# Longer score runs, and DMA transposes in place of TensorE transposes, in a fused attention and squared-ReLU kernel

## The chip, the cores and the metric

The kernel runs on one core of a Trainium2 chip. Times are device microseconds of one execution of the whole program; the median of several runs is the time of a kernel. The core has a matrix engine (PE), a vector engine (DVE), an activation engine (ACT), a general engine (POOL) and a queue engine (SP). In this program POOL issues the loads from HBM, and SP issues the constants and the stores. All of these DMAs run on the same 16 DMA engines.

## The reference

Eight batches, eight heads, 576 positions, head width 64. Attention with a bias that depends only on the distance of two positions, then a two-layer network with a squared ReLU on every token:

```python
scores = q @ k^T / 8 + bias_table[bucket(|i - j|)]        # 8 x 8 x 576 x 576
attn   = softmax(scores)
x      = (attn @ v), heads side by side                   # 4608 tokens x 512
out    = relu(x @ w_in) ** 2 @ w_out                      # 512 -> 2048 -> 512, fp32
```

All distances of 128 and more share one bucket. So only a band around the diagonal needs a factor of its own, and the kernel multiplies exp(score) by a small table there.

## The kernel before, in words

The work is cut in 32 **pairs**: pair p is batch p/4 and heads 2·(p%4) and the next one. The two heads lie on the two halves of the 128 partitions.

- **Loads.** q and k of a batch are loaded into a staging buffer `stg` (two of them), positions on the partitions, and cast to fp16. v goes to `vas` and `v4s`.
- **Turning q and k.** `pair` turns them with five 128x128 PE transposes each (L504) into a PSUM bank of the ring `g_ps` (three banks). ACT or DVE copies the bank to `qts` and `kts` (L483, L485).
- **Scores.** For each block of 128 keys (four blocks) and each half of 288 queries, two matmuls of 64x128 tiles, one per head, write one of two PSUM sets `sets_ps` (L528). The 64 last keys take four matmuls of 64x64 tiles (L535). ACT takes the exponential of each set into `pts` or `p4s` (L554), two buffers of each. DVE multiplies the band by the table (L574).
- **Attention times v** ("PV"): five tiles of 128 queries in two parts (three and two tiles). Each tile is one matmul of 130 columns (L612) and eight of 65 (L619). DVE divides by the sum (L636, L641) and writes `xs`.
- **Turning x.** After the four pairs of a batch `x_turn` turns x with 20 PE transposes (L663) into `xt_sb`, again through `g_ps` and a copy.
- **The network** runs over nine groups of 512 tokens. The first layer has 16 chunks of four 512-column matmuls (`f1`, L758), each followed by a ReLU on ACT (L778) and a square on DVE (L786). The second layer has four output tiles of 16 matmuls (`f2`, L707), each followed by a copy (L727 or L733) and a store (L741). `f1` and `f2` use the same three PSUM banks as the transposes.

Scores use PE as two arrays of 64 rows, and the 64 last keys as 64x64 arrays. Everything else uses it as one array of 128x128. The planner calls these modes "r", "q" and "f".

The order of all instructions is written out by a planner, `Plan.schedule`, when the program is built. It places each step on its engine at the earliest time its inputs and buffers allow, with assumed costs (`mm`, `act`, `dve`), assumed delays between engines (`LAT`), an assumed cost of a change of PE mode (`SWITCH`), and due times (`nominal`, and `due` in `layers`) as a tie break. The chip then runs each engine's instructions in that order.

## Time and profile before

| | |
|---|---|
| three runs | 442.41, 442.55, 440.94 us; median 442.41 us |
| the profiled execution's own time | 443.17 us |
| its span, first to last instruction | 441.4 us |
| busy: PE, ACT, DVE, POOL | 417.2, 288.0, 210.2, 119.5 us |
| granted PE clock, mean | 0.996 |
| first `f1` matmul starts | 50.24 us |
| last matmul ends | 437.6 us |

The profile is of one execution. A group row names a line of the kernel, an engine, an operation, its tiles and its count; then the busy time, the mean length of one, and the idle time of the engine just before. The length of one matmul in it is the time from start to end, and several are in flight at once, so what a matmul costs is read from the distance between starts. The windows view has one row for each stretch of time, with busy time by engine, granted clock and the mean share in which the 16 DMA engines were busy. The timeline view gives start, length and count of instructions in order of time.

### The profile page before, as it was taken

To read this page: it belongs to the slowest core of one execution; us is meant where nothing else is said; L and a number is where in the kernel's file an instruction comes from. 1 tells how busy PE (TensorE), PEld (TensorE's weight loads), DVE (VectorE), ACT (ScalarE), POOL (GpSimd) and SP (SyncE) were. 2 spreads that over 40 slices of the span, in tenths; PEclk is the share of its full clock that TensorE was granted. 3 is DMA by queue.
4 is the path that set the end of the run, shared out by engine and by line. 5 is a ranking of instruction groups with operands and counts; after the bars stand their busy time and mean duration, and the time that the engine had idled before them with its cause. 6 is when DMAs were issued, how large, how long until landed. Compare 5 with 4: busy or idle time off the path is not lost.

```text
span 441.4 us, 9092 instructions
## 1 busy us (share of the span) xinstructions
PE 417.2 (95%) x3713; PEld 209.7 (48%) x3713; DVE 210.2 (48%) x513; ACT 288.0 (65%) x495; POOL 119.5 (27%) x154
## 2 busy tenths in 40 slices
PE   1687999999999999999999999999999999999996
PEld 0265545554455445544454445544454454544442
DVE  3545556445555655455455446465544553352210
ACT  1657787667866876777767666685777766464421
POOL 7998569422162205230254007000000000000000
PEclk9998999999999999999999999999999999999999
DMA  9999999918091808980099009400010001000111
GB/s 131 159 87 165 190 166 122 137 29 76 2 133 28 74 1 74 108 55 24 26 133 79 1 25 113 68 1 25 25 50 1 25 24 49 25 25 25 48 49 72
DMA packets 122170, 29.24 MB, mean 66 GB/s; under 512 B 113896, under 2 KB 117008, under 8 KB 122128
## 3 DMA queue, kind: packets, MB, share of 16 engines
q0 software_dynamic: 115552, 18.36, 56.5%
q1 hardware_dynamic: 6576, 10.30, 6.7%
q8 instruction: 29, 0.48, 0.5%
q14 instruction: 13, 0.11, 0.1%
HBM read 37.55 MB, written 9.45 MB: 106 GB/s over the span
## 4 chain that ended last, share of the span: by engine, by line
PE 91%; DMA 3%; ACT 3%; DVE 2%; issue 1%; SPq 0%; ACTq 0%; DVEq 0%
PE f L707 30%; PE f L758 29%; PE st L528 11%; PE pv L619 9%; PE f L504 4%; PE pv L612 3%; PE st L535 3%; PE f L663 2%; ACT pt L554 2%; DMA tr_sb<-t_bias 1%; DMA t_bias<-tv_sb 1%; DMA oh_sb<-c_oh 1%; SPq L243 0%; DVE pt L574 0%; ACT y L727 0%
## 5 line engine op out<-in xcount | busy, mean ns | idle before, releaser
L554 ACT ACTIVATE pt<-st 128x576 f16<-128x576 f32 x256 | 157.3, 649 | 42.1 <-PE st L528 40.1
L707 PE MATMUL f<-w_out_sb,g 128*128 128x512 f16 x576 | 144.9, 380 | 0.4 <-ACT qt L483 0.3
L758 PE MATMUL f<-xt,w_in_sb 128*128 128x512 f16 x576 | 141.0, 380 | 0.9 <-DVE xt L485 0.4
L778 ACT ACTIVATE rt<-f 128x512 f16<-128x512 f32 x144 | 86.1, 598 | 57.1 <-PE f L758 53.2
L786 DVE TENSOR_TENSOR g<-rt 128x512 f16<-128x512 f16 x144 | 61.1, 425 | 100.6 <-ACT rt L778 100.4
L758 PEld LDWEIGHTS <-w_in_sb 128*128 128x128 f16 x576 | 51.0, 97 | 61.3 <-issue 3.8
L574 DVE TENSOR_TENSOR pt<-pt,tb_sb 128x512 f16<-128x512 f16 (+2 forms) x96 | 59.7, 623 | 40.7 <-ACT pt L554 37.7
L707 PEld LDWEIGHTS <-g 128*128 128x128 f16 x576 | 48.7, 98 | 60.8 <-issue 13.2
L528 PE MATMUL st<-qt,kt 64*128 64x288 f16 x512 | 66.2, 298 | 4.8 <-ACT pt L554 3.7
L243 POOL DMA_DIRECT2D qs<-in_q_dram x47 | 38.1, 834 | 101.4 <-PE f L504 98.1
L619 PE MATMUL pv<-va,pt 128*128 128x65 f16 x1280 | 57.2, 196 | 0.2 <-DVE pt L574 0.2
L619 PEld LDWEIGHTS <-pt 128*128 128x128 f16 x1280 | 52.6, 100 | 5.1 <-issue 0.7
L528 PEld LDWEIGHTS <-kt 64*128 64x128 f16 x512 | 20.2, 94 | 57.8 <-issue 52.9
L243 POOL DMA_DIRECT2D va<-in_v_dram x32 | 28.4, 916 | 43.0 <-PE pv L619 26.9
L243 POOL DMA_DIRECT2D ks<-in_k_dram x47 | 38.2, 858 | 6.3 <-DMA w_out_sb<-in_moe_w_out_dram 3.5
L612 PE MATMUL pv<-vm,pm 128*128 128x130 f16 x160 | 36.1, 225 | 0.2 <-DVE x L641 0.2
L641 DVE TENSOR_TENSOR x<-pv,r 128x384 f16<-128x384 f32 x64 | 31.4, 491 | 2.2
L554 ACT ACTIVATE pm<-st 128x576 f16<-128x576 f32 x32 | 20.8, 651 | 13.0 <-PE st L535 13.0
L636 DVE RECIPROCAL r<-pv 128x6 f32<-128x6 f32 x64 | 11.9, 187 | 26.0 <-PE pv L619 25.7
L727 ACT ACTIVATE y<-f 128x512 f32<-128x512 f32 x20 | 12.0, 598 | 18.6 <-PE f L707 18.2
L504 PE MATMUL f<-id_sb,qs 128*128 128x128 f16 x160 | 15.5, 234 | 4.3 <-DMA qs<-in_q_dram 4.3
L612 PEld LDWEIGHTS <-pm 128*128 128x128 f16 x160 | 15.9, 99 | 6.5 <-issue 1.4
(37 smaller groups left out, 175.7 us busy)
## 6 DMA issues: line engine op xcount, KB each, us to landing
out_dram<-y SPq DMA_DIRECT2D x36, 256.0 KB, 2.0
va<-in_v_dram POOLq DMA_DIRECT2D x32, 128.0 KB, 5.2
qs<-in_q_dram POOLq DMA_DIRECT2D x28, 128.0 KB, 4.6
ks<-in_k_dram POOLq DMA_DIRECT2D x28, 128.0 KB, 5.1
w_in_sb<-in_moe_w_in_dram POOLq DMA_DIRECT2D x4, 512.0 KB, 7.4
w_out_sb<-in_moe_w_out_dram POOLq DMA_DIRECT2D x4, 512.0 KB, 9.5
qs<-in_q_dram POOLq DMA_DIRECT2D x15, 64.0 KB, 4.8
ks<-in_k_dram POOLq DMA_DIRECT2D x15, 64.0 KB, 4.7
```

Source lines behind the costliest of these rows:

```text
L243: lambda: io(eng.dma_start(out=out_(), in_=in_())),
L504: io(nc.tensor.transpose(ps[:, ts(t, 128)], stg[b_stg[b].slot][w][:, t, ts(hp, 128)], id_sb))
L528: nc.tensor.matmul(ps[:, e, 0:HQ], kt[rows, ts(jt, 128)], qt[rows, ts(hh, HQ)], start=True, stop=True,)
L554: nc.scalar.activation(out=dst, in_=sets_ps[st.slot][:, :, 0:HQ], func=EXPF, scale=SCALE)
L574: io(nc.vector.tensor_tensor(out=a, in0=a, in1=t, op=MULT))
L612: nc.tensor.matmul(ps[:, i, :, :], pm[:, c : c + 128], vm[:, hp, :, 0:65], start=True, stop=False)
L619: nc.tensor.matmul(ps[:, i, e, :], pt[:, (2 * jt + e) * S + c : (2 * jt + e) * S + c + 128], va[:, jt, 2 * hp + e, 0:65], start=False, sto ...
L641: nc.vector.tensor_tensor(out=xs[xb.slot][:, qt0 : qt0 + nq, ts(hp, 128)].rearrange("p t (e d) -> p t e d", e=2), in0=ps[:, :, :, 0:64], i ...
L707: nc.tensor.matmul(g_ps[bank.slot], gs[gb.slot][:, nt, ts(m, 128)], w_out_sb[:, nt, :], start=(nt == 0), stop=(nt == 15),)
L758: nc.tensor.matmul(g_ps[bank.slot], w_in_sb[:, kk, ts(nt, 128)], xt_sb[:, kk, c : c + GT], start=(kk == 0), stop=(kk == 3),)
L778: nc.scalar.activation(out=rts[rb.slot], in_=g_ps[bank.slot], func=RELUF)
L786: nc.vector.tensor_tensor(out=gs[gb1.slot][:, nt, :], in0=rts[rb.slot], in1=rts[rb.slot], op=MULT)
```

## The change

The scores of a pair are asked for in fewer and longer pieces. A step `run` multiplies one or two blocks of 128 keys with the first 512 queries at once: two 512-column matmuls of 64x128 tiles per block. From batch 1 on a pair has two such runs, of two key blocks each, and a run takes both PSUM sets together. In batch 0 it has four runs of one block. The remaining 64 queries and 64 keys are computed with the whole array: `spread` copies them into zeroed 128x128 tiles `qzs` and `kzs`, one head in each diagonal corner. `last_queries` then takes four matmuls of 128 columns and `last_keys` two of 288. The exponentials follow: four of 1024 elements per partition, one of 576 and one of 512 per pair, in place of nine of 576.

q and k of batches 2 to 7 are turned by `dma_start_transpose` on SP, from the staging buffer to `qts` and `kts`, five blocks of 128x128 in one DMA. Each part of x is turned by a DMA transpose of three or two blocks as soon as it is divided, from `xs` to `xt_sb`. q and k of batches 0 and 1 are loaded six positions to a partition and turned by PE in 12 transposes of 96 x 64, two beside each other.

The layouts of `stg`, `xs` and `xt_sb` follow this: `xt_sb` holds four batches, and the group of 512 tokens that wraps round its end is computed in two halves of 256 columns. The bias table is staged in a buffer of the network's hidden layer. The loads come in another order: q and k of batch 0 first, the weights later. q and k of batches 2 to 7 are loaded by 20 DMAs a batch in place of 10. The planner gets other costs and due times.

```diff
-XR = 2560
+XR = 4 * S
+DT_QK = 2
+PERIOD, LEAD, FAST, FASTN = 9800.0, 10600.0, 4700.0, 5
+AHEAD, G0, GP = 12700.0, 38500.0, 37900.0
+DT_X = True
...
-LAT = {"PE": 200.0, "ACT": 90.0, "DVE": 90.0, "POOL": 120.0, "DMA": 0.0, "SP": 0.0}
-SWITCH = 60.0
+LAT = {"PE": 200.0, "ACT": 90.0, "DVE": 90.0, "POOL": 120.0, "DMA": 1800.0, "SP": 0.0, "XB": 2000.0}
+SWITCH = 105.0
...
-        t = 0.0
+        t, taken = 0.0, {}
         for b in op.bufs:
             if b.slot is None:
-                if not b.ring.free:
+                i = taken[b.ring] = taken.get(b.ring, -1) + 1
+                if len(b.ring.free) <= i:
                     return float("inf")
-                t = max(t, min(b.ring.free)[0])
+                t = max(t, sorted(b.ring.free)[i][0])
         return t
...
-    NSTG, NQK, NPT, NV, NX, NGB, NRT, NY = 2, 5, 2, 3, 2, 2, 4, 3
-    stg = [[sb(f"{n}s{i}", [128, 5, 512]) for n in "qk"] for i in range(NSTG)]
-    qts = [sb(f"qt{i}", [128, S]) for i in range(NQK)]
-    kts = [sb(f"kt{i}", [128, S]) for i in range(NQK)]
+    NSTG, NQK, NPT, NV, NX, NGB, NRT, NY = 2, 4, 2, 3, 2, 2, 4, 3
+    stg = [[sb(f"{n}s{i}", [128, 6 * 512]) for n in "qk"] for i in range(NSTG)]
+    qts = [sb(f"qt{i}", [128, 640]) for i in range(NQK)]
+    kts = [sb(f"kt{i}", [128, 640]) for i in range(NQK)]
+    qzs = [sb(f"qz{i}", [128, 128]) for i in range(NQK)]
+    kzs = [sb(f"kz{i}", [128, 128]) for i in range(NQK)]
...
-    xs = [sb(f"x{i}", [128, 5, 512]) for i in range(NX)]
-    xt_sb = sb("xt", [128, 4, XR])
+    xs = [sb(f"x{i}", [128, 4, 5, 128]) for i in range(NX)]
+    xt_sb = sb("xt", [128, 4, XR + 64])
     gs = [sb(f"g{i}", [128, 16, GT]) for i in range(NGB)]
+    tr_sb = gs[1][:, 0:6, :].rearrange("p a b -> p (a b)").rearrange("p (h w) -> p h w", h=H)
...
+    def load_six(b, w, h0, nh):
+        src = (q, k)[w]
+        l = load(
+            "POOL", nc.gpsimd,
+            lambda: six(stg[b_stg[b].slot][w])[:, h0 : h0 + nh, :],
+            const(src[b, h0 : h0 + nh].rearrange("h (p j) d -> p h (j d)", j=6)),
+            96 * nh * 107, (), [b_stg[b]], pdue(),
+        )
+        for hp in range(h0 // 2, (h0 + nh) // 2):
+            l_qk[b, w, hp] = [l]
...
+        for hp in range(4):
+            l_qk[b, w, hp] = tails + [
+                load(
+                    "POOL", nc.gpsimd,
+                    lambda hp=hp, e=e: rows(stg[b_stg[b].slot][w])[:, hp, 0:4, ds(64 * e, D)],
+                    const(src[b, 2 * hp + e, 0:512, :].rearrange("(t p) d -> p t d", p=128)),
+                    512 * 34.5, first, [b_stg[b]], pdue(),
+                )
+                for e in range(2)
+            ]
...
     for hp in range(4):
         for w in range(2):
-            load_pair(0, w, hp)
+            load_six(0, w, 2 * hp, 2)
         if hp == 1:
-            load_v(0)
+            load_v_tail(0, range(4))
+            for h in range(4):
+                load_v_head(0, h)
+    for h in range(4, 8):
+        load_v_head(0, h)
+    for u in range(4):
+        load_w_in(u)
     for w in range(2):
-        load_qk(1, w)
-    for kk in range(4):
-        load_w_in(kk)
+        load_six(1, w, 0, 4)
     load_v(1)
+    for w in range(2):
+        load_six(1, w, 4, 4)
     for u in range(4):
         load_w_out(u)
...
-    PERIOD, LEAD, FAST = 10300.0, 12000.0, 5900.0
-
     def nominal(p):
-        return LEAD + FAST * min(p, 5) + PERIOD * max(p - 5, 0)
-
-    xt_ready = {}
+        return LEAD + FAST * min(p, FASTN) + PERIOD * max(p - FASTN, 0)
...
-        after = max(0.0, T - 9000.0)
+        after = max(0.0, T - AHEAD)
         qb = Buf(r_qk)
         evac = []
         for w, dst in ((0, qts), (1, kts)):
+            if b >= DT_QK:
+                o = P.add(
+                    {"SP": 1250.0},
+                    lambda w=w, dst=dst: io(
+                        nc.sync.dma_start_transpose(
+                            out=dst[qb.slot].rearrange("p (t d) -> p t d", d=128), in_=rows(stg[b_stg[b].slot][w])[:, hp].rearrange("p t d -> p (t d)")
+                        )
+                    ),
+                    l_qk[b, w, hp], [qb, b_stg[b]], T - 6000, after,
+                )
+                evac.append(P.add({"XB": 800.0}, None, [o], [qb, b_stg[b]], T - 6000))
+                continue
...
-                for t in range(5):
-                    io(nc.tensor.transpose(ps[:, ts(t, 128)], stg[b_stg[b].slot][w][:, t, ts(hp, 128)], id_sb))
-
-            o = P.add({"PE": 5 * mm(128)}, tr, l_qk[b, w, hp] + [l_id], [bank, b_stg[b]], T - 3000, after, "f")
...
+                if b < SIX:
+                    for j in range(6):
+                        for e in range(2):
+                            io(
+                                nc.tensor.transpose(
+                                    ps[ds(64 * e, 64), ts(j, 96)], six(t)[:, 2 * hp + e, ts(j, D)],
+                                    id_sb[0:96, 0:96],
+                                )
+                            )
+                else:
...
+        spread = []
+        for w, src, dst in ((0, qts, qzs), (1, kts, kzs)):
+            for e in range(2):
+                rw = ds(64 * e, 64)
+
+                def sp(o, src=src, dst=dst, rw=rw):
+                    eng = nc.vector if o.eng == "DVE" else nc.gpsimd
+                    io(eng.tensor_copy(out=dst[qb.slot][rw, rw], in_=src[qb.slot][rw, 512:576]))
+
+                spread.append(one_of({"DVE": 130.0, "POOL": 300.0}, sp, [evac[w]] + z_fix, [qb], T - 1000))
...
-        for jt in (4, 0, 1, 2, 3):
-            for half in range(2) if jt < 4 else (0,):
...
-                o = P.add(
-                    {"PE": mm(HQ) + 10 if jt < 4 else 2 * mm(HQ) + 10},
-                    score, evac, [st, qb], T, after, "r" if jt < 4 else "q",
-                )
...
+        def run(jts):
+            sets = [Buf(r_set) for _ in jts]
+
+            def score():
+                kt, qt = kts[qb.slot], qts[qb.slot]
+                for jt, st in zip(jts, sets):
+                    for e in range(2):
+                        rw = ds(64 * e, 64)
+                        io(
+                            nc.tensor.matmul(
+                                sets_ps[st.slot][:, e, :], kt[rw, ts(jt, 128)], qt[rw, 0:512],
+                                start=True, stop=True,
+                            )
+                        )
+
+            o = P.add({"PE": len(jts) * mm(512) + 10}, score, evac, sets + [qb, pb], T, after, "r")
+            for jt, st in zip(jts, sets):
+
+                def ex(jt=jt, st=st):
                     io(
                         nc.scalar.activation(
-                            out=dst, in_=sets_ps[st.slot][:, :, 0:HQ], func=EXPF, scale=SCALE
+                            out=p5(pts[pb.slot])[:, jt, :, 0:512], in_=sets_ps[st.slot], func=EXPF, scale=SCALE
                         )
                     )
 
-                exps[jt, half] = P.add({"ACT": act(2 * HQ)}, ex, [o], [st, pb], T)
+                exps[jt] = P.add({"ACT": act(1024)}, ex, [o], [st, pb], T)
...
+        def last_queries():
+            st = Buf(r_set)
+
+            def score():
+                for jt in range(4):
+                    io(
+                        nc.tensor.matmul(
+                            sets_ps[st.slot][:, 0, ts(jt, 128)], kts[qb.slot][:, ts(jt, 128)], qzs[qb.slot],
+                            start=True, stop=True,
+                        )
+                    )
+
+            o = P.add({"PE": 4 * mm(128)}, score, evac + spread[0:2], [st, qb, pb], T, after, "f")
...
+        def last_keys():
+            st = Buf(r_set)
+
+            def score():
+                for half in range(2):
+                    io(
+                        nc.tensor.matmul(
+                            sets_ps[st.slot][:, half, 0:HQ], kzs[qb.slot], qts[qb.slot][:, ts(half, HQ)],
+                            start=True, stop=True,
+                        )
+                    )
+
+            o = P.add({"PE": 2 * mm(HQ)}, score, evac + spread[2:4], [st, qb, pb], T, after, "f")
...
+        if b < 1:
+            run([0])
+            run([1])
+            last_keys()
+            run([2])
+            run([3])
+        else:
+            run([0, 1])
+            last_keys()
+            run([2, 3])
+        last_queries()
...
             o = P.add(
-                {"PE": nq * (8 * 56.0 + 60.0)}, pv,
-                bands + list(exps.values()) + l_v[b] + first[4:], [bank, pb, b_v[b]], T + 1, after, "f",
+                {"PE": nq * 300.0}, pv,
+                bands + list(exps.values()) + l_v[b, hp] + first, [bank, pb, b_v[b]], T + 1, after, "f",
...
+            if DT_X:
+                c = (b % 4) * S + 128 * qt0
+                t = P.add(
+                    {"SP": 1000.0},
+                    lambda qt0=qt0, nq=nq, c=c: io(
+                        nc.sync.dma_start_transpose(
+                            out=xt_sb[:, hp, c : c + 128 * nq].rearrange("p (t d) -> p t d", d=128), in_=xs[xb.slot][:, hp, qt0 : qt0 + nq, :].rearrange("p t d -> p (t d)")
+                        )
+                    ),
+                    [o, x_last.get((hp, 1 - part))] + xt_free(b * S + 128 * (qt0 + nq)), [xb], T - 2000,
+                )
+                t = x_last[hp, part] = P.add({"XB": 160.0 * nq}, None, [t], [xb], T - 2000)
...
     def xt_free(upto):
 
         old = upto - 1 - XR
-        return [f1_last[old // GT]] if old >= 0 and old // GT in f1_last else []
+        return [f1_last[old // GT]] if old >= 0 else []
...
-        due = 30000.0 + 40000.0 * g
+        due = G0 + GP * g
...
-                            {"PE": 4 * mm(512)}, f2, d + squares[g - 1] + l_wout, [bank, gb], 1e6, 0.0, "f"
+                            {"PE": 4 * mm(512)}, f2, d + squares[g - 1][4 * part : 4 * part + 4] + [l_wout[part]], [bank, gb], 1e6, 0.0, "f"
...
-                    for kk in range(4):
-                        io(
-                            nc.tensor.matmul(
-                                g_ps[bank.slot], w_in_sb[:, kk, ts(nt, 128)], xt_sb[:, kk, c : c + GT],
-                                start=(kk == 0), stop=(kk == 3),
+                    n = min(GT, XR - c)
+                    for a, z, c in ((0, n, c), (n, GT, 0)):
+                        for kk in range(4 if z > a else 0):
+                            io(
+                                nc.tensor.matmul(
+                                    g_ps[bank.slot][:, a:z], w_in_sb[:, kk, ts(nt, 128)],
+                                    xt_sb[:, kk, c : c + z - a],
+                                    start=(kk == 0), stop=(kk == 3),
+                                )
                             )
-                        )
...
-                    {"PE": 4 * mm(512)}, f1, xt_ready[g] + l_win, [bank], due + i * 2000, 0.0, "f"
+                    {"PE": 4 * mm(512)}, f1, xt_ready[g] + [l_win[nt // 4]], [bank], due + i * 2000, 0.0, "f"
...
-                        [r], [rb, gb1], due - 1e5,
+                        [r] + ([t for ts_ in l_tab for t in ts_] if g == 1 else []), [rb, gb1], due - 1e5,
...
-        x_turn(b, norms)
+        if not DT_X:
+            x_turn(b, norms)
```

The order of PE in the middle of the program (rows that repeat the one above them are left out). `kt` and `qt` are the turned k and q of a pair, `st` a PSUM set of scores, `f` a bank of the network. Before, one half of a key block, then a chunk of the network, then the last keys:

```order
L528 LDWEIGHTS kt_82
L528 MATMUL st_110<-qt_77,kt_82 128x288
L758 LDWEIGHTS w_in_sb
L758 MATMUL f_114<-xt,w_in_sb 128x512
L535 LDWEIGHTS kt_83
L535 MATMUL st_111<-qt_78,kt_83 64x288
L758 LDWEIGHTS w_in_sb
L758 MATMUL f_113<-xt,w_in_sb 128x512
L528 LDWEIGHTS kt_83
L528 MATMUL st_110<-qt_78,kt_83 128x288
```

And of the changed kernel, one run between two chunks:

```order
L897 LDWEIGHTS w_in_sb
L897 MATMUL f_120<-xt,w_in_sb 128x512
L604 LDWEIGHTS kt_80
L604 MATMUL st_115<-qt_76,kt_80 128x512
L604 LDWEIGHTS kt_80
L604 MATMUL st_116<-qt_76,kt_80 128x512
L897 LDWEIGHTS w_in_sb
L897 MATMUL f_118<-xt,w_in_sb 128x512
```

The two key blocks of a run now stand side by side and fill both sets. Over the whole program PE changes its mode 381 times in the order before and 144 times in the changed one.

PE where the network begins, before: the transposes of x of batch 0 stand right ahead of the first matmul of `f1`.

```order
L663 LDWEIGHTS x_96
L663 MATMUL f_113<-id_sb,x_96 128x128
L663 LDWEIGHTS x_96
L663 MATMUL f_114<-id_sb,x_96 128x128
L758 LDWEIGHTS w_in_sb
L758 MATMUL f_115<-xt,w_in_sb 128x512
```

And in the changed kernel:

```order
L741 LDWEIGHTS pt_92
L741 MATMUL pv_117<-va_95,pt_92 128x65
L897 LDWEIGHTS w_in_sb
L897 MATMUL f_118<-xt,w_in_sb 128x512
```

Nothing of PE stands between the last PV matmul of batch 0 (L741) and the first `f1` (L897); the DMA transposes of x run in between.

SP's queue in the middle of the program held only stores before:

```order
L741 DMA out_dram<-y_105 128x512
L741 DMA out_dram<-y_106 128x512
L741 DMA out_dram<-y_107 128x512
```

And now (`qs` and `ks` are the staging buffers):

```order
L542 DMA_TRANSPOSE kt_79<-ks_74 128x5x128
L779 DMA_TRANSPOSE xt<-x_101 128x3x128
L878 DMA out_dram<-y_112 128x512
L542 DMA_TRANSPOSE kt_80<-ks_74 128x5x128
L779 DMA_TRANSPOSE xt<-x_101 128x2x128
L878 DMA out_dram<-y_110 128x512
L542 DMA_TRANSPOSE qt_77<-qs_73 128x5x128
```

The 36 stores share the queue with 48 transposes of q and k and 64 of x, and stand behind them in its order.

238 lines of the change are left out of this document (119 added, 119 removed).

## The prediction

> **What bounds the kernel now.** I read the page first: who is busy, in which slices, and who the chain of work that ended last belongs to.
>
> ```profile
> span 441.4 us, 9092 instructions
> PE 417.2 (95%) x3713; PEld 209.7 (48%) x3713; DVE 210.2 (48%) x513; ACT 288.0 (65%) x495; POOL 119.5 (27%) x154
> PE   1687999999999999999999999999999999999996
> PEclk9998999999999999999999999999999999999999
> PE 91%; DMA 3%; ACT 3%; DVE 2%; issue 1%; SPq 0%; ACTq 0%; DVEq 0%
> ```
>
> PE is the bound from the fifth slice to the last. Its clock is full nearly throughout. Then the windows, cut at the start of the first `f1` (50.24 us) and at the end of the last matmul:
>
> ```profile
> 0.00:50.24 50.24, 31.34 (x358) 19.98 (x358) 25.19 (x77) 28.14 (x48) 42.05 (x60) 0.97 1.47 140
> 50.24:437.60 387.36, 385.87 (x3356) 189.73 (x3356) 185.02 (x437) 259.28 (x447) 77.41 (x95) 1.00 0.53 57
> 50.24:381.96 331.72, 330.24 (x3100) 164.68 (x3100) 171.83 (x406) 235.97 (x408) 77.41 (x95) 1.00 0.61 60
> ```
>
> There are two regimes. Until 50 us PE waits for much; after that it idles 1.5 us in 387 (387.36 less 385.87). So in the second, a microsecond of PE work removed is a microsecond gained, unless something else becomes late. What PE's work costs I take from distances between starts in its timeline:
>
> ```profile
> 47.30 0.22 PE L612 MATMUL pv<-vm,pm 128*128 128x130 f16 x1
> 47.60 0.22 PE L612 MATMUL pv<-vm,pm 128*128 128x130 f16 x1
> 52.93 0.42 PE L528 MATMUL st<-qt,kt 64*128 64x288 f16 x4
> 53.28 1.90 PE L758 MATMUL f<-xt,w_in_sb 128*128 128x512 f16 x8
> 201.11 0.30 PE L528 MATMUL st<-qt,kt 64*128 64x288 f16 x2
> 201.34 1.04 PE L758 MATMUL f<-xt,w_in_sb 128*128 128x512 f16 x4
> 202.30 0.30 PE L528 MATMUL st<-qt,kt 64*128 64x288 f16 x2
> 378.92 0.38 PE L663 MATMUL f<-id_sb,x 128*128 128x128 f16 x4
> 379.14 1.03 PE L758 MATMUL f<-xt,w_in_sb 128*128 128x512 f16 x4
> 422.75 14.84 PE L707 MATMUL f<-w_out_sb,g 128*128 128x512 f16 x68
> ```
>
> The last row gives 0.216 us per 512-column matmul (14.84 less the last one's own 0.38, over 67). Two pairs of score matmuls take 0.35 us until the next chunk starts (52.93 to 53.28), one pair 0.23 (201.11 to 201.34). So a pair costs 0.12: both heads stream their 288 columns together, and 0.11 remains for the change of mode back. A chunk of four takes 0.96 until the next scores start (201.34 to 202.30) where 4 x 0.216 are 0.86: 0.10 for the change into the mode. A query tile of PV is 0.30 (47.30 to 47.60), a transpose 0.055 (378.92 to 379.14, four).
>
> By these, all of PE's work is 1152 x 0.216 = 248.8 (network), 320 pairs of score matmuls x 0.12 = 38.4, 160 x 0.30 = 48.0 (PV) and 480 x 0.055 = 26.4 (transposes): 361.6 us. In the order PE changes mode 381 times; at 0.105 that is 40. Together 401.6, where the chain has PE at 91% of 441.4 = 401.7. The model holds.
>
> **The change part by part.**
>
> *Mode changes.* 381 fall to 144, counted in the order. Two prices: 0.105 from the rows above; and, from the long window, 387.36 less 1.5 idle less 345.0 of work (361.6 less the 16.6 that the order, at these prices, has ahead of the first `f1`), over 354 changes: 0.116. I take 0.11: 237 x 0.11 = **-26.1** (bounds -24.9, -27.5).
>
> *Score matmuls.* 128 pairs of 512 columns x 0.216 = 27.6; 128 `last_queries` of 128 columns at the transpose's 0.055 = 7.0; 64 `last_keys` of 288 at 0.12 = 7.7. Sum 42.3 for 38.4: **+3.9**. The long runs cost columns; they save switches.
>
> *PE transposes.* 480 fall to 192 of 96 columns. Scaled by columns from 0.055 they are 0.041 each. They cost 3.9 if two run beside each other as the scores do, 7.9 in series. I take 4: 26.4 becomes 4.0, **-22.4** (or -18.5). The group that wraps adds 64 matmuls of half length to replace as much work: nothing.
>
> *What moves to DMA.* 112 transposes on SP: 48 of five blocks and 64 of two or three, 400 blocks of 32 KB, 13.1 MB. No transpose on DMA is in this trace. The nearest rows:
>
> ```profile
> q0 software_dynamic: 115552, 18.36, 56.5%
> out_dram<-y SPq DMA_DIRECT2D x36, 256.0 KB, 2.0
> id_sb<-c_id SPq DMA_DIRECT2D x1, 32.0 KB, 7.6
> ```
>
> One takes between 2.0 us (a 256 KB store) and 7.6 (a 32 KB constant under the loads of the start). As rows of 256 bytes they are 51,200 packets; at q0's price (56.5% of 441.4 us x 16 engines over 115,552 packets, 34.5 ns) they are 110 us of the 16 engines, 0.33 of the 332 us window on top of its 0.61. The share went to 1.47 in the first window, so there is room. [...] q and k are asked for up to a pair ahead, about 10 us, so 2.0 to 7.6 is hidden; I cost it at nothing. If it takes longer, the first step late is a pair's `run` and PE behind it. Behind a waiting transpose on SP stand the stores, then the copies `y`, then a bank of the network.
>
> [...]
>
> *Copies.* ACT and DVE lose 84 copies out of PSUM, DVE and POOL gain 128 of 64x64, `spread`. DVE (48%) and POOL (27%) hide them; without that cover `last_queries` waits, with the PV behind it. The 60 further load issues on POOL, 0.86 us each, lie in its idle 73%.
>
> ```profile
> L554 ACT ACTIVATE pt<-st 128x576 f16<-128x576 f32 x256 | 157.3, 649 | 42.1 <-PE st L528 40.1
> L778 ACT ACTIVATE rt<-f 128x512 f16<-128x512 f32 x144 | 86.1, 598 | 57.1 <-PE f L758 53.2 <-DVE x L641 2.3
> L554 ACT ACTIVATE pm<-st 128x576 f16<-128x576 f32 x32 | 20.8, 651 | 13.0 <-PE st L535 13.0
> L243 POOL DMA_DIRECT2D ks<-in_k_dram x47 | 38.2, 858 | 6.3 <-DMA w_out_sb<-in_moe_w_out_dram 3.5 <-PE f L758 1.7 <-DMA va<-in_v_dram 0.6
> ```
>
> *ACT.* 64 more elements cost 51 ns (649 less 598), so 1024 cost 598 + 8 x 51 = 1006. A pair takes 4 x 1.006 + 0.651 + 0.598 = 5.3 us in place of 5.8. ACT's share stays near 70%, but its pieces grow and a run needs both sets free: the wait that can be new. Bounds: nothing (PE has network chunks to do meanwhile), or one exponential, 1.0, at each of 56 runs after the start, 56 us. Before, with sets taken singly, such waits summed to 3.7 us; near that end I take **+5**.
>
> ```profile
> PE st L528 <- ACT pt L554: 3.7, 12, 0.7
> 10.40 0.69 PE L504 MATMUL f<-id_sb,qs 128*128 128x128 f16 x5 [4.34 <-DMA qs<-in_q_dram]
> 19.59 0.41 DVE L574 TENSOR_TENSOR pt<-pt,tb_sb 128x512 f16<-128x512 f16 x1
> ```
>
> *The start.* q now comes ahead of the weights, so PE can begin before 10.4. But the tables come no earlier (first band 19.59), so the first PV cannot start before about 22, nor, with two `pt` buffers, the third pair's exponentials before about 24.5. Two pairs of these, 10.5, the last bands, PV and division, about 4, and the landing of x, 3 (at least 2.0), give the first `f1` at 42; bounds 38 and the present 50. What counts is the time without work ahead of it: now 50.2 less 16.6 of work less 27 changes (3.0) = 30.6; then 42 less 14.0 of work less 26 changes (2.9), both counted in the new order, = 25.1. **-5.5** (bounds -9.5, +2.5).
>
> Sum against the profiled execution's own 443.2 us: -26.1 + 3.9 - 22.4 + 5 - 5.5 = -45.1, 398.1. The median of the runs lies 0.8 below that execution: **397 us**.
>
> **The rivals.**
>
> *ACT sets the pace.* Each run waits half an exponential that no chunk covers: 56 x 0.5 = 28 in place of 5, 420 us. For it: ACT must do 28 pairs x 5.3 plus 128 ReLUs x 0.6 and some 16 of copies, 241 us, in an attention stage that shrinks to about 285. Against it: the order puts chunks of the network between runs nearly everywhere.
>
> *The start gains nothing.* x of batch 0 lands late, as `id_sb` did with 7.6 us, and the first `f1` stays at 50: 405 us.
>
> *The transposes take turns.* If the DMA engines turn one block at a time, the 400 blocks form a chain from about 25 us to the network's last stretch, which is 59 us before the end. It overtakes the present 443 at (443 - 25 - 59) / 400 = 0.90 us a block; at 1.0 us it gives 484. For it: the 32 KB constant with 7.6 us, and that nothing here shows several transposes at once. Against it: a store of eight times the bytes lands in 2.0 us. [...]
>
> That the mode changes do not vanish is no rival: they are in the order.
>
> **How the numbers follow.** Forecast 0.60 (its own range 387 to 410), late start 0.10, ACT 0.18, transposes in turn 0.12. A change under 0.5% is about what this kernel's measurement cannot tell. Faster takes the first two and nine tenths of ACT's, 0.86; ACT's upper end and the remainder leave 0.02 for the same; slower 0.12. The range 385 to 428 holds the forecast, the late start and most of ACT's case: about 8 in 10.
>
> **What would show it.** Right: a run between two chunks, 0.86 of matmuls and 0.2 of mode changes; PE idle after the first `f1` below 10 us; that `f1` near 42; transposes landing below 8 us. Wrong: PE idle ahead of L604 charged to ACT (first rival) or to DMA `qt` and `kt`, with landing times that grow along the program (third); idle ahead of the first L897 charged to `xt` (second). The forecast is wrong in its base if PE's mode changes cost more or less than 0.11 at the new places.

## The result, and the profile after

| | before | after |
|---|---|---|
| median of the runs | 441.77 us (440.94 to 442.55, 4 runs) | 419.94 us (415.49 to 422.35, 4 runs) |
| the profiled execution: its own time, span | 443.17, 441.4 us | 420.58, 418.6 us |
| PE idle within the span | 24.2 us | 40.5 us |
| mean granted PE clock | 0.996 | 0.974 |
| first `f1` matmul; `f1` without further stops from | 50.24; 50.24 us | 39.52; 48.94 us |

The change makes the kernel faster: 0.9472 of the time before (95% interval 0.9393 to 0.9552). That is about 22 us, half of the 45 that were forecast, and the time lies within the range on record. The ratios here and below leave out executions in a slower state of the chip, here the one of 422.35 us; the medians count them. The page of the changed kernel, its span, PE's row of busy times, the slices of PE and of its clock, and the chain by engine:

```profile
span 418.6 us, 8453 instructions
PE 378.1 (90%) x3297; PEld 199.7 (48%) x3297; DVE 197.7 (47%) x540; ACT 263.7 (63%) x374; POOL 152.9 (37%) x242
PE   4586398687899959999999999999999999999996
PEclk9998599999899998999999999999999999999999
PE 75%; DMA 13%; POOL 7%; issue 2%; ACT 1%; DVE 1%; SPq 0%; ACTq 0%; POOLq 0%
```

PE is still the bound from the middle on, but no longer from 50 us. DMA and POOL, which had 3% and nothing of the chain, now have 20%. The windows show it in two rows for each kernel. In a row stand the stretch, its length, then busy time of PE, PEld, DVE, ACT and POOL, the clock, the DMA share and GB/s. Before:

```profile
0.00:200.00 200.00, 180.51 (x1772) 94.44 (x1772) 105.48 (x268) 137.75 (x237) 97.88 (x128) 0.99 1.07 96
200.00:400.00 200.00, 199.11 (x1772) 98.41 (x1769) 98.77 (x232) 137.11 (x236) 21.57 (x26) 1.00 0.31 40
```

After, the same halves and the stretch behind the start:

```profile
0.00:200.00 200.00, 163.48 (x1568) 86.65 (x1568) 101.73 (x296) 123.71 (x171) 117.07 (x179) 0.95 1.28 130
200.00:400.00 200.00, 200.00 (x1664) 106.64 (x1663) 95.56 (x244) 136.45 (x198) 35.79 (x64) 1.00 0.54 75
48.94:414.00 365.06, 349.42 (x2959) 182.53 (x2959) 172.60 (x447) 238.57 (x342) 124.13 (x198) 0.99 0.81 93
```

In the second half nothing waits. All the loss is in the first: 36.5 us without PE work there, in place of 19.5. Behind the first free `f1` the idle time is 365.06 less 349.42, 15.6 us. The waits of PE in that stretch (us in total, times, longest; the first row counts the wait of 5.0 that ends as the stretch begins):

```profile
PE f L897 <- DMA xt<-x: 11.3, 3, 5.0
PE st L653 <- POOL kz L586: 2.9, 1, 2.9
PE pv L734 <- DVE x L763: 1.5, 3, 0.9
PE st L604 <- ACT pm L663: 1.5, 3, 0.8
```

Where the 441.4 us of span went can be put into three sums. I multiply PE's busy time by the granted clock, slice by slice of 5 us: this is the work at full clock. (In the changed kernel, from 49.32 to 51.45 us at a granted clock of 0.50, the weight loads of 512-column matmuls follow each other at 0.43 us, where a matmul at full clock takes 0.216.) Busy time above it is lost to the clock, and the rest of the span is idle.

| us | before | after | difference | forecast |
|---|---|---|---|---|
| PE work at full clock | 415.9 | 372.9 | -43.0 | -44.6 (mode changes, scores, transposes) |
| lost to a low clock | 1.3 | 5.2 | +3.9 | 0 |
| PE idle | 24.2 | 40.5 | +16.3 | -0.5 (start -5.5, waits +5) |
| span | 441.4 | 418.6 | -22.8 | -45.1 |

So the removed work came out about as predicted, and half of the gain was paid back in waits (16.3 us) and in low clock (3.9).

### The profile page after: what moved, and what is told of

Its sections match the earlier page's. It is cut to its first block, busy times and chain, and to the rows that moved or that the text cites. A ratio compares the mean times of both kernels' runs of the same rounds, so it can differ in the third digit from the quotient of the medians.

```text
span 418.6 us, 8453 instructions
## 1 busy us (share of the span) xinstructions
PE 378.1 (90%) x3297; PEld 199.7 (48%) x3297; DVE 197.7 (47%) x540; ACT 263.7 (63%) x374; POOL 152.9 (37%) x242
## 4 chain that ended last, share of the span: by engine, by line
PE 75%; DMA 13%; POOL 7%; issue 2%; ACT 1%; DVE 1%; SPq 0%; ACTq 0%; POOLq 0%
PE f L844 29%; PE f L897 27%; PE pv L741 8%; PE st L604 6%; DMA va<-in_v_dram 4%; DMA w_out_sb<-in_moe_w_out_dram 4%; POOL va L250 3%; DMA w_in_sb<-in_moe_w_in_dram 3%; DMA xt<-x 3%; PE pv L734 2%; POOL ks L250 2%; PE st L653 1%; PE st L628 1%; POOL qs L250 1%; ACT pt L615 1%
## 5 line engine op out<-in xcount | busy, mean ns | idle before, releaser
L897 PE MATMUL f<-xt,w_in_sb 128*128 128x512 f16 (+1 forms) x640 | 143.4, 367 | 14.3 <-DMA xt<-x 14.1
L615 ACT ACTIVATE pt<-st 128x1024 f16<-128x1024 f32 x128 | 126.0, 1022 | 32.8 <-PE st L604 32.6
L844 PE MATMUL f<-w_out_sb,g 128*128 128x512 f16 x576 | 137.7, 379 | 0.0
L897 PEld LDWEIGHTS <-w_in_sb 128*128 128x128 f16 x640 | 60.9, 99 | 77.5 <-issue 17.0
L844 PEld LDWEIGHTS <-g 128*128 128x128 f16 x576 | 53.2, 98 | 64.4 <-issue 8.7
L741 PE MATMUL pv<-va,pt 128*128 128x65 f16 x1280 | 58.2, 197 | 2.8 <-DVE pt L696 2.7
L741 PEld LDWEIGHTS <-pt 128*128 128x128 f16 x1280 | 53.3, 100 | 11.1 <-issue 3.6
L250 POOL DMA_DIRECT2D qs<-in_q_dram x66 | 47.2, 752 | 13.7 <-DMA w_out_sb<-in_moe_w_out_dram 8.2
L250 POOL DMA_DIRECT2D ks<-in_k_dram x66 | 47.5, 793 | 4.4 <-DMA ks<-in_k_dram 3.2
L604 PE MATMUL st<-qt,kt 64*128 64x512 f16 x256 | 42.8, 399 | 5.5 <-ACT pt L615 2.4
L586 POOL COPY qz<-qt 64x64 f16<-64x64 f16 x27 | 7.1, 265 | 99.1 <-DMA qt<-qs 93.4
L638 ACT ACTIVATE pt<-st 128x512 f16<-128x512 f32 x32 | 19.1, 597 | 5.2 <-PE st L628 4.6
```

Source lines behind the costliest of these rows:

```text
L250: lambda: io(eng.dma_start(out=out_(), in_=in_())),
L604: nc.tensor.matmul(sets_ps[st.slot][:, e, :], kt[rw, ts(jt, 128)], qt[rw, 0:512], start=True, stop=True,)
L615: nc.scalar.activation(out=p5(pts[pb.slot])[:, jt, :, 0:512], in_=sets_ps[st.slot], func=EXPF, scale=SCALE)
L741: nc.tensor.matmul(ps[:, i, e, :], pt[:, (2 * jt + e) * S + c : (2 * jt + e) * S + c + 128], va[:, jt, 2 * hp + e, 0:65], start=False, sto ...
L844: nc.tensor.matmul(g_ps[bank.slot], gs[gb.slot][:, nt, ts(m, 128)], w_out_sb[:, nt, :], start=(nt == 0), stop=(nt == 15),)
L897: nc.tensor.matmul(g_ps[bank.slot][:, a:z], w_in_sb[:, kk, ts(nt, 128)], xt_sb[:, kk, c : c + z - a], start=(kk == 0), stop=(kk == 3),)
```

## The experiments

All ratios are to the kernel before, on the same chip. The same three sums for each of the profiled executions:

| kernel | median, us | ratio (95%) | work | low clock | idle |
|---|---|---|---|---|---|
| e1, runs only | 422.73 | 0.956 (0.954 to 0.959) | 394.0 | 4.3 | 23.0 |
| e2, q and k by DMA | 414.95 | 0.937 (0.933 to 0.941) | 379.4 | 5.5 | 28.5 |
| e3, x by DMA | 422.57 | 0.957 (0.953 to 0.960) | 384.5 | 2.7 | 31.6 |
| changed kernel, both | 419.94 | 0.947 (0.939 to 0.955) | 372.9 | 5.2 | 40.5 |
| e4, x of batch 0 on PE | 411.24 | 0.929 (0.925 to 0.934) | 370.9 | 7.4 | 28.6 |
| e4b, x of batches 0 and 1 | 410.54 | 0.930 (0.928 to 0.932) | 372.5 | 1.7 | 34.1 |
| e5, planner's latency 7.0 | 419.02 | 0.948 (0.945 to 0.951) | 369.9 | 9.2 | 40.4 |
| e6b, e4 with single runs | 406.21 | 0.918 (0.914 to 0.922) | 375.4 | 0.0 | 26.8 |
| e7, e4 with `spread` on DVE | 408.37 | 0.925 (0.922 to 0.927) | 372.7 | 4.5 | 28.4 |
| e9, e6b with `spread` on DVE | 406.76 | 0.919 (0.914 to 0.924) | 375.6 | 0.0 | 26.4 |
| e11, e9, long runs from batch 2 | 404.55 | 0.916 (0.912 to 0.921) | 374.1 | 0.0 | 27.0 |
| e10, order of loads | 422.57 | 0.959 (0.952 to 0.965) | 369.3 | 9.4 | 41.9 |
| e12, loads held | 412.89 | 0.933 (0.928 to 0.937) | 372.0 | 8.8 | 31.4 |

**The parts apart: e1, e2, e3.** The theory was that the landing of the x transposes (8.2 us in the start, where 3 were assumed) is what ate the gain; the rival, that the runs' waits on ACT did.

```diff
-DT_QK = 2            # e1 and e3: q and k of all batches on PE
+DT_QK = 8
-DT_X = True          # e1 and e2: x of all batches on PE
+DT_X = False
```

> The changed kernel with every transpose back on PE: q and k of batches 2 to 7 by five 128x128 transposes, x by 20 a batch. The score runs, the loads and the order rules stay. PE's work by the prediction's prices: 367.8 us and 144 mode changes, 383.6 with 0.11 each, against 403.9 before and 361.6 of the changed kernel. Theory A (the x of a batch lands late by DMA, and PE waits and then runs at a low clock; the rest of the prediction holds): no wait for xt, the first f1 near 40, all else beside PE's work about 33 us (start 25, tail 4, small waits 4): 417 us, the same as the changed kernel within 1%. Theory B (the long runs themselves lose, waiting for both score sets): PE idle in front of the score runs as in the changed kernel or more, 425 to 435. Theory C (the mode changes are worth less than 0.11): above 430 with little idle.

> The changed kernel with x alone back on PE (20 transposes a batch, copies by ACT and DVE); q and k of batches 2 to 7 stay on DMA. PE's work with mode changes 370.4 us, 8.8 more than the changed kernel. Theory A (late x): the 14.1 us of waits for xt and most of the low clock behind them go, 8.8 of work comes: 404 to 408 us, faster than the changed kernel by 3%. Rival (the transposes on DMA slow the loads and each other, so that any of them costs): PE still waits for qt and kt, 415 or more.

> The changed kernel with q and k of batches 2 to 7 back on PE; x stays on DMA. PE's work with mode changes 374.8 us, 13.2 more than the changed kernel. Theory A (late x): the waits for xt stay, somewhat shorter where q and k stood ahead of x in SP's queue: 426 to 432 us, slower than the changed kernel by 2 to 3%. Rival (q and k by DMA are what is late): 415 or less.

All three missed the numbers of the theory, e1 by 6 us above, e2 by 7 above its range and e3 by 3 below, yet the order of the parts is clear. e2 lies where its rival began (415), but PE waits for neither `qt` nor `kt` in its trace. The longer runs, with the new loads and the new plan that e1 keeps, are worth 19 us; PE's work fell by 21.9 there, where the prices in the expectation said 20.3 (403.9 to 383.6). Turning q and k by DMA on top adds 8. Turning x by DMA too takes 5 back (e2 to the changed kernel; the intervals just overlap), and on its own it is worth nothing (e1 to e3), although it takes 9.5 us of work from PE. The start shows why. First free `f1` of e2, and then the same place in e3:

```profile
41.06 8.79 PE L897 MATMUL f<-xt,w_in_sb 128*128 128x512 f16 x40 [0.28 <-ACT xt L522]
```

```profile
43.02 0.61 PE L897 MATMUL f<-xt,w_in_sb 128*128 128x512 f16 x1 [2.87 <-DMA xt<-x]
48.19 6.28 PE L897 MATMUL f<-xt,w_in_sb 128*128 128x512 f16 x21 [4.56 <-DMA xt<-x]
```

The number in brackets is idle time of PE ahead of the row and what ended it. With x on PE, 40 matmuls run through from 41.06; by DMA PE stops twice, and then 21 matmuls take 6.28 us where 21 x 0.216 are 4.5: the granted clock was 0.50 from 40 to 50 us and 0.86 from 50 to 55.

**Only batch 0's x back on PE: e4, e4b.**

```diff
-DT_X = True
+DT_X = 1             # e4b: 2
...
-            if DT_X:
+            if b >= DT_X:
...
-        if not DT_X:
+        if b < DT_X:
```

> The changed kernel with x of batch 0 alone turned by PE. PE's work 0.9 us more. Theory A: the first f1 then starts near 41 and runs on without the 7.8 us of waits for xt at 39 to 49 us, and at full clock: 408 to 412 us; the later waits for xt (6.3 us) stay. Rival (the start is held by something else, as the weights or the tables): the first f1 still runs freely only from about 48, 418 to 421 us.

> x of batches 0 and 1 turned by TensorE, of batches 2 to 7 by DMA; the counts give 1.3 us more of TensorE's work than with x of batch 0 alone there (411.2 us). Theory A, with x of batch 0 on TensorE the waits for xt are gone (0.6 us in all), so the second batch only costs its work: 412 to 413. Rival B, the transposes of batch 1 also hold up SP and the loads in 95 to 107 us: 407 to 410.

e4 gave 411.24, inside the theory's range: 9 us less than the changed kernel, for 0.9 us more of PE work in the order. First the start of e4, then its wait for x by DMA over the whole program:

```profile
38.80 8.79 PE L897 MATMUL f<-xt,w_in_sb 128*128 128x512 f16 x40 [0.46 <-ACT xt L522]
```

```profile
PE f L897 <- DMA xt<-x: 0.6, 1, 0.6
```

In e4's order the DMA transposes of batches 1 to 7 are hidden; those that the first layer had stood waiting for are on PE. The expectation let the later waits of 6.3 us stay and the clock be full. The trace has 0.6 us of such waits and loses 7.4 us to the clock, so the range was met in part by two errors of opposite sign. Other orders do wait for later x: 2.4 us in e4b, 5.9 in e12. The second batch on PE (e4b) brings 0.7 us within intervals that overlap: neither expectation is told apart. Its trace has other waits at other places, as the next row shows, where e4 had 2.4 us on the same kind of copy:

```profile
PE st L628 <- POOL qz L586: 5.4, 1, 5.4
```

**Was it the planner's belief? e5.** The planner assumes 2.0 us from a transpose to its use.

```diff
-LAT = {..., "XB": 2000.0}
+LAT = {..., "XB": 7000.0}
```

> The planner's latency of a DMA transpose raised from 2.0 to 7.0 us (LAT, L76), all else as in the changed kernel (419.9 us). Theory A, the waits for xt behind the start (4.2 us at 106, 2.2 us at 157, in all 6.3) come from the planner counting on a landing of 2 us where the trace shows 6 to 8: they go, with the low clock behind them, the start does not move: 412 to 415 us. Rival B, the transposes are late because SP and the loads hold them, whatever the planner believes: 418 to 421. Rival C, the later due times push score runs and projections apart and new waits come: over 421.

419.02 is the number of rival B, but not its reason. Both waits for x behind the start, 6.3 us, are gone, as theory A said. In their place PE waits for other inputs, and the low clock costs 9.2 us in place of 5.2. So the planner's belief decides what PE waits for, and the sum stays. The first row is the start, the other two are the new waits:

```profile
50.85 0.61 PE L897 MATMUL f<-xt,w_in_sb 128*128 128x512 f16 x1 [5.87 <-DMA xt<-x]
78.56 0.58 PE L628 MATMUL st<-qz,kt 128*128 128x128 f16 x4 [5.98 <-POOL qz L586]
110.45 1.04 PE L604 MATMUL st<-qt,kt 64*128 64x512 f16 x4 [5.66 <-DMA kt<-ks]
```

**Why the landing is slow: e10, e12.** In the changed kernel the x transposes of the start are the slowest to land: the median is 8.2 us until 60 us, 6.1 from 60 to 100, and 2.3 to 3.6 in the four stretches of 60 us from 120 to 360. Issue to landing (minimum, median, maximum) until 60 us, and from 300 to 360 us:

```profile
DMA to landing us min/median/max: 7.4/8.2/8.9
...
DMA to landing us min/median/max: 2.3/2.3/4.3
```

In the first stretch the loads fill the 16 DMA engines (share 1.44 until 48.94 us). To test that as the cause, e10 moved the loads of `w_out` and of batches 2 to 7 behind the transposes of batch 0 in the plan:

```diff
+        if b == 0:
+            gate[0] = list(x_last.values())     # dependence in the plan
+            for u in range(4):
+                load_w_out(u)
+            ... loads of batches 2 to 7, with the same dependence
```

> The changed kernel (419.9 us), with the loads of w_out and of batches 2 to 7 held on GpSimd until the last x transpose of batch 0 has landed; TensorE's order is nearly the same. Theory A, the x transposes of batch 0 take 8.2 us (median) because they share the DMA engines with those loads: from about 38 us on the queue drains, the last ones land in 3 to 5 us, the first layer runs freely from 44 to 46 us in place of 48.94, total 414 to 417. Rival B, they take long for another reason (the queue of SP, the form of the transpose): 48 to 49 us as before, 419 to 422. What is held comes later, w_out near 58 us where it is wanted at 74.

It does not answer the question, since the dependence in the plan made no wait on the chip: the first load of `w_out` went out at 37.02 us, while the transposes were still being issued. What it did show is the price of POOL's queue. A `kz` copy stands behind a load of k that itself waits for an earlier load, and PE waits 6.1 us for the copy:

```profile
36.07 0.67 POOL L250 DMA_DIRECT2D ks<-in_k_dram  x1 [1.10 <-DMA ks<-in_k_dram]
36.78 0.23 POOL L581 COPY kz<-kt 64x64 f16<-64x64 f16 x1
37.02 0.75 POOL L250 DMA_DIRECT2D w_out_sb<-in_moe_w_out_dram  x1
```

```profile
37.07 0.66 PE L648 MATMUL st<-qt,kz 128*128 128x288 f16 x2 [6.10 <-POOL kz L581]
```

(The lines of e10 are 5 lower than in the changed kernel, those of e12 7 lower.) e12 makes the loads wait through data, with a copy that reads every transpose and writes where `w_out` will land:

```diff
+        if b == 0:
+            hold = lambda: io(nc.gpsimd.tensor_copy(
+                out=w_out_sb[:, 0:4, 0:2], in_=xt_sb[:, :, 0:512:384]))
+            gate.append(P.add({"POOL": 300.0}, hold, list(x_last.values()), (), pdue()))
+            ... q and k of heads 4 to 7 of batch 1, w_out, batches 2 to 7
...
-one_of({"DVE": 130.0, "POOL": 300.0}, sp, ...)
+one_of({"DVE": 130.0}, sp, ...)
```

> The changed kernel (419.9 us) with a copy on GpSimd that reads a column of every x transpose of batch 0 and writes where w_out will land, so that q and k of heads 4 to 7 of batch 1, w_out and all later loads truly wait for those transposes (the run that held them by the plan alone did not: its first load of w_out went out at 37 us). All spread copies are on VectorE, so that none queues behind the held loads; that edit alone gave 2.8 us on another kernel. Theory A, the landing of 8.2 us comes from sharing the DMA engines with the loads: the transposes issued last land in 2.3 to 4 us, the first layer runs freely from 42 to 45 us (48.94 before). Rival B, the transposes are slow by themselves or by SP: 7 to 8 us, freely from 48 to 49. The total is 410 to 416 by A and 416 to 420 by B, both with the danger that the held loads make batch 1 late.

The first layer now runs freely from 42.81, as theory A said, though at a low clock (0.50 from 40 to 45 us, 0.63 from 45 to 50). Landing of the four transposes issued after 33 us, first in the changed kernel, then in e12:

```profile
DMA to landing us min/median/max: 7.8/8.3/8.9
```

```profile
DMA to landing us min/median/max: 2.3/4.5/7.1
```

The four issued before 33 us, with the loads still under way, have a median of 7.3 in e12 and 7.7 in the changed kernel. PE in e12 at that place:

```profile
41.46 0.61 PE L890 MATMUL f<-xt,w_in_sb 128*128 128x512 f16 x1 [0.83 <-DMA xt<-x]
42.81 7.58 PE L890 MATMUL f<-xt,w_in_sb 128*128 128x512 f16 x21 [0.74 <-DMA xt<-x]
```

So the same transposes, issued at the same times (22.4 to 40.5), land sooner once the loads are gone: the last four have a median of 4.5 us in place of 8.3, and the quickest takes 2.3. From 40 to 45 us the DMA share is 0.39 in e12 and 1.60 in the changed kernel. The load on the DMA engines is the cause; how an engine divides its time between the loads and the transposes no run shows. Of the 7 us that the median fell, about 3 may come from `spread` on DVE, which was changed as well (e7).

**The long runs: e6b, e9, e11.** What remained was whether the mode changes are worth 0.11 each.

```diff
-        if b < 1:            # the runs of one key block
+        if True:             # e6b and e9; e11: if b < 2
```

> The kernel with x of batch 0 on TensorE (411.2 us), with runs of one key block each for all batches in place of the longer runs of batches 1 to 7: mode changes 142 to 187, the same matmuls. Theory A, a change of mode costs 0.11 us wherever it stands: +5.0, 416 us (415 to 418). Rival B, changes are hidden beside waits or the loads of weights: 411 to 412. Rival C, shorter runs ask the exponentials for less at a time, and the waits on them (7 us in that kernel) go: 406 to 410.

e6b fell on the side of the third reading, and at its better end: 5 us faster than e4 (406.21, the intervals apart) with 45 mode changes more. Its waits on ACT did not shrink, though (10.9 us in all, e4 9.8), so the reason given there does not hold. What shrank are the lost clock, 7.4 us to nothing, and the wait for `qz`. The windows around 60 us, e4 first, then e6b:

```profile
56.00:60.00 4.00, 2.35 (x24) 1.18 (x24) 1.69 (x4) 4.00 (x7) 4.00 (x7) 0.94 1.37 89
60.00:66.00 6.00, 5.81 (x87) 4.48 (x86) 3.16 (x10) 3.77 (x7) 6.00 (x8) 0.50 1.74 112
```

```profile
56.00:60.00 4.00, 2.29 (x34) 1.48 (x34) 2.26 (x5) 4.00 (x6) 4.00 (x7) 1.00 1.36 90
60.00:66.00 6.00, 4.69 (x106) 3.16 (x104) 5.81 (x14) 5.50 (x8) 6.00 (x8) 1.00 1.93 111
```

Both had idled 1.7 us of the four before. In e4 the granted clock was then 0.50 for six us (5.81 us of busy time for 87 matmuls), in e6b it was 1.00 (4.69 for 106): nearly equal idle stretches ended differently. Chance from one execution to the next is not seen: all four of e4 have a mean clock of 0.979, those of e6b 0.992 to 0.999. What brings the clock down in e4's order stays open.

> The kernel with x of batch 0 on TensorE (411.2 us), with all spread copies of q and k (L586) on VectorE, none on GpSimd. Theory A, the wait of 2.4 us for qz at 67 to 70 us, and its like in other stretches, comes from a copy that stands on GpSimd behind the issues of the next loads: it goes, 408 to 410 us. Rival B, VectorE takes 25 copies more (6 us) in the stretch where the divisions of x are already waited for: 411 to 414.

e7 (the edit of `spread` shown with e12, on e4) gave 408.37: the wait on POOL is gone, and 2.9 us with it, at the edge of the intervals.

> x of batch 0 on TensorE, runs of one key block for all batches (that was 406.2 us), and all spread copies on VectorE. No wait for POOL qz stands in the trace of the kernel without this edit, so theory A: 405 to 407, no gain. Rival B, VectorE's 30 copies more make the divisions late: 407 to 410. Its trace should again show a granted clock of 1.00 in nearly all slices if the low clock came from the longer runs' waits; if the low clock is back at 60 to 70 us, the 4 to 7 us that it cost elsewhere are chance of the order.

> The kernel above (runs of one key block, spread on VectorE), with runs of two blocks only from batch 2 on: mode changes 187 to 149, the same matmuls. Theory A, a change of mode costs 0.11 to 0.12 and the longer runs only hurt in batch 1, where the network has too few chunks to put between: 38 x 0.115 = 4.4 us below the kernel above, 401 to 403 us. Rival B, longer runs make waits on ACT in every batch that eat the saving: 405 to 408.

e9 is e6b again within its noise, and its trace has the full clock again (mean 0.999). e11, with long runs only where the network has chunks to spare, is the best kernel of the study at 404.55 us, between its two expectations. Its gain over e9 (38 fewer changes, 2.2 us) is less than their intervals can tell. Its clock is full in the trace too (mean 0.999), with long runs in batches 2 to 7. Whether those of batch 1 bring it down (e4 loses 7.4 us, e7 4.5, e4b 1.7) no run tests by itself. In its trace and e9's the work differs by 1.5 us, 0.04 a change. The rows of the changed kernel between chunks, where nothing waits, still give the price of the forecast:

```profile
252.11 0.61 PE L604 MATMUL st<-qt,kt 64*128 64x512 f16 x4
252.65 1.92 PE L897 MATMUL f<-xt,w_in_sb 128*128 128x256 f16 x16
...
256.40 0.39 PE L628 MATMUL st<-qz,kt 128*128 128x128 f16 x4
256.62 2.78 PE L897 MATMUL f<-xt,w_in_sb 128*128 128x256 f16 x24
259.33 0.61 PE L604 MATMUL st<-qt,kt 64*128 64x512 f16 x4
```

From 252.11 to 252.65 are 0.54 for two pairs (0.43) and a change (0.11); from 256.62 to 259.33 are 2.71 for 24 halves (2.59) and a change (0.12). Between e4 and e6b the work rises by 4.5 us for 45 changes, 0.10 each; between e7 and e9 by 2.9. Why whole kernels give 0.04 to 0.10 and rows 0.11 is open; the work at full clock is worked out from slices and is uncertain by one or two us.

## Why the prediction was half right

**The work of PE: right.** The three terms said -26.1 + 3.9 - 22.4 = -44.6, and PE's work fell by 43.0. The runs cost what they were priced at: the rows above give 0.54 for a run of two blocks, and 0.22 for four `last_queries` matmuls (0.055 each). The transposes of 96 columns lay between the two readings, neither fully beside each other nor in series:

```profile
55.07 0.70 PE L559 MATMUL f<-id_sb,qs 96*64 96x96 f16 x24
55.82 1.46 PE L897 MATMUL f<-xt,w_in_sb 128*128 128x512 f16 x6
```

24 take 0.75 us, 0.031 each, so the 192 cost 6 and not 4. One number of the prediction contradicts its own sum: among the signs of being right it gives a run "0.86 of matmuls", but two blocks are two pairs at 0.216, and the rows show 0.43.

**The start: the term that failed.** It said "the landing of x, 3 (at least 2.0)" and the first `f1` at 42. The last division of batch 0 ends at 40.4, where the sum had 39. `f1` runs freely 8.5 us later, from 48.94, and -5.5 became about +1.4 (48.94 less 14.0 and 2.9, against 30.6). Had the landing been 3, the step would about have held: in e12, where the last ones land sooner, the time is 42.81. The lower bound came from stores of 2.0 us, the median of 36 over the whole program, and the value taken was near it. The row with 7.6 us, a 32 KB constant under the loads of the start, was quoted beside it and describes the very conditions that batch 0's transposes met.

**"q and k are asked for up to a pair ahead ... so 2.0 to 7.6 is hidden; I cost it at nothing": wrong for x, right for q and k.** PE waits 6.3 us for x behind the start (11.3 less the 5.0 in front of it), and in no row of its waits for `qt` or `kt` by DMA. x has no such lead: a group of 512 tokens needs all four heads of a batch, so the last transpose stands between the last division and the first layer. SP adds to that. The last x of batch 1 is divided by 96.4, but its transpose stands behind a `qt` transpose and two stores:

```profile
96.56 0.53 SPq L878 DMA_DIRECT2D out_dram<-y  x1
97.27 1.29 SPq L542 DMA_TRANSPOSE qt<-qs  x1
98.94 0.34 SPq L878 DMA_DIRECT2D out_dram<-y  x1
99.37 2.11 SPq L779 DMA_TRANSPOSE xt<-x  x1
```

It is issued by 101.5, and the first layer resumes only at 106.5, with 4.2 us of PE idle ahead of it. The prediction named what queues behind a waiting transpose on SP; it did not ask what an x transpose queues behind.

**"DVE (48%) and POOL (27%) hide them": not quite.** A `kz` copy on POOL stood behind 11 us of load issues and cost PE 2.9 us:

```profile
65.32 1.58 POOL L250 DMA_DIRECT2D ks<-in_k_dram  x2
66.78 3.61 POOL L250 DMA_DIRECT2D va<-in_v_dram  x4
70.25 1.39 POOL L250 DMA_DIRECT2D vm<-in_v_dram  x2
71.48 3.69 POOL L250 DMA_DIRECT2D va<-in_v_dram  x4
75.06 1.35 POOL L250 DMA_DIRECT2D vm<-in_v_dram  x2
76.45 0.70 POOL L586 COPY qz<-qt 64x64 f16<-64x64 f16 x3
77.21 0.52 POOL L586 COPY kz<-kt 64x64 f16<-64x64 f16 x2
```

The 60 additional load issues were costed at nothing on POOL's mean share, and that share was no cover in this stretch, where the issues fill POOL from 65.32 to 76.45.

**ACT: right.** Waits on the exponentials behind the start are 4.3 us of the 15.6, where the forecast had +5; the first rival's 28 us did not come, since chunks stand between the runs. That the total landed at the 420 us of that rival is chance: its wait is not in the trace.

**The clock: not thought of.** 3.9 us more than before. The granted clock is 0.50 from 40 to 50 us, while PE waits for x, and 0.75 from 48.94 to 55.00, where 21 matmuls take 6.20 us in place of 4.5. It is down already ahead of the first wait for x (0.84 from 35 to 40 us), so not all of this belongs to x. With x of batch 0 on PE (e4) it is 1.00 from 35 to 55 us, but 0.50 from 60 to 66.

**The other rivals.** The transposes do not take turns at 0.9 us a block: a `qt` transpose issued at 105.09 and one at 107.76, each of five blocks, with `kt` transposes between them 1.3 us apart, land within 2.6 to 3.4 us, at most 0.7 a block. "The start gains nothing" had the right cause, x landing late, and its price of 8 us is near what the start itself lost, 6.9 (+1.4 for -5.5). It lacked the rest of the 22: the clock, the later batches and the copies on POOL.

**Its own signs.** Of the signs that it named for being right three failed: PE idles 15.6 us behind the first free `f1` and not below 10, that `f1` stands at 48.94 and not near 42, and transposes land in up to 8.9 us and not below 8. The price of a mode change held. The sign of the second rival was there, idle time ahead of the first L897 charged to `xt`. That the time lies in the range is owed to the width that was laid in for the rivals, not to the step that the forecast had for the start.

**Sum.** Against the forecast span of 396.3 (441.4 less 45.1) the 418.6 are 22.3 more: 1.6 of work, 9.1 of idle time behind the start (15.6 for 1.5 + 5), 7.7 in the start and at the end, and 3.9 of clock. e11, with x of batch 0 on PE, `spread` on DVE and single runs in batch 1, has a span of 401.1, no low clock and 27.0 us of idle time: 17.5 of the 22.3 are back. The other 4.8 are 3.3 of idle time and 2.8 of work above the forecast, less the 1.3 that the forecast left to the clock.

## What to carry to other kernels

Price a transfer by the row that was measured under the load it will meet (the x transposes landed in a median of 8.2 us beside the loads of the start, and of 2.3 from 300 to 360 us), and ask first which transfers stand between a last producer and a first consumer with no other work between them: those few belong on the engine that is waiting (here one batch's x on PE gave 9 us back), the others may go by DMA (in e4 PE waits 0.6 us for them). When work is taken off the bound engine, expect waits to appear where the program is thin (here its first batches: 36.5 us without PE work in the first 200, in place of 19.5), and count with a lower clock beside and behind them (here 0.50 from 40 to 50 us, 0.75 from 48.94 to 55.00). Share of an engine is no cover: here a copy of 0.2 us on POOL, 37% busy over the span, stood behind 11 us of load issues, and PE waited 2.9 us for it.

## What the runs showed of the hardware that was not expected

- A DMA transpose from SBUF to SBUF of two to five blocks of 128x128 holds SP for about 1.2 us per issue, in a few for up to 2.4. It lands 2.3 us (x) and 2.6 us (q, k) after its issue in quiet stretches, 7.4 to 8.9 us beside the loads of the start.
- Several such transposes are under way at once: issues 1.3 us apart with landings of 2.6 to 5.1 us.
- Behind a stretch of 9 us with 1.2 us of work (40.00 to 48.94), at a granted clock of 0.50, 21 matmuls of 512 columns took 6.20 us in place of 4.5 (0.75 from 48.94 to 55.00). Behind nearly equal idle stretches (1.7 us of four before 60 us) the granted clock was 0.50 in e4 and 1.00 in e6b from 60 to 66 us.
- 96 x 64 transposes laid in two halves of the array cost 0.031 us each, against 0.055 for a 128x128 one.
